# Halving the first input block by tokens over two DMA queues, and evacuating the first transposes in two pieces

## Chip, cores, metric

One core of a Trainium2 chip. The metric is device time in microseconds (us) of one execution, median of several. Times of the profiler's own span are about 1.8 us shorter than the device time and are used only to compare profiles.

## The reference, cut to what matters

Four layers on x of shape (1, 2048, 1024) in bf16: linear attention, gated MLP, and both again, each behind a layer norm.

```python
x = x + _A_ref(_layernorm(x), A_wqkv, A_wo)      # 32 heads, phi(q), phi(k), linear attention
x = x + _B_ref(_layernorm(x), B_W_gate, B_W_up, B_W_down)
...                                              # the same two once more
```

Only the very start matters here: the first tokens of x must be loaded, normalized, transposed, and multiplied with the first columns of `wqkv`.

## The kernel before

x is worked on in blocks of 128 tokens (one token per partition, 1024 columns). The head of the kernel loads block 0 in two column halves, one on SP's DMA queue and one on ScalarE's, and keeps TensorE (PE) busy with dummy matmuls meanwhile:

```python
def head(self):
    ...
    zero = self.ep.tile([P, NW], BF16, tag="e")
    nc.vector.memset(zero, 0.0)
    idle = self.ps3.tile([P, NW], F32, tag="b")
    for _ in range(12):
        nc.tensor.matmul(idle, lhsT=zero[:, 0:P], rhs=zero, start=True, stop=True)

    k0, k1, v0, q0, q1 = (ring.place() for _ in range(5))
    self.load_x(0, 0)                    # block 0, columns 0..511, SP's queue
    self.load_x(0, 1, nc.scalar)         # block 0, columns 512..1023, ScalarE's queue
    k0(0, H)                             # first half of the first weight block, SP
    self.load_x(1, None, nc.scalar)      # block 1, whole, ScalarE's queue
    k0(H, 2 * H)
    self.load_x(2)
    k1()
    ...
```

`k0(0, H)` is 512 rows of 1 KB, `load_x(1)` 128 rows of 2 KB. Four 128x128 transposes go into one PSUM tile, which is then copied to SBUF ("evacuated") by VectorE or ScalarE. The order of the first block on VectorE and ScalarE is written out by hand. `stat` takes the statistics of one half of a block, `rstd` makes the mean and the reciprocal standard deviation of them (VectorE's aggregate, then two steps on ScalarE), `scale` normalizes, `turn` transposes:

```python
def turn(j, h):
    tp = self.ps3.tile([P, H, P], BF16, tag="b")
    for i in range(H):
        kt = h * H + i
        nc.tensor.transpose(tp[:, i, :], xn[j][:, kt * P:(kt + 1) * P], self.ident)
    dst = self.xnT[0, 0][:, h * H:(h + 1) * H, j * P:(j + 1) * P]
    ...                                  # take(engine): copy tp to dst

def block0():
    stat(0, 0)                           # block 0: statistics of both column halves
    stat(0, 1)
    rstd(0)
    stat(1, 0)                           # block 1 stands ahead of block 0's scaling
    scale(0, 0)
    scale(0, 1)
    t0 = turn(0, 0)
    t1 = turn(0, 1)
    t0("s")
    stat(1, 1)
    rstd(1)
    t1("v")
    k(0, 0, between)                     # 8 matmuls; block 1's transposes after the sixth
```

## Time and profile before

| | before |
|---|---|
| device time, first three runs | 1629.09 us (1628.83 to 1629.37) |
| PE busy in the profiled span | 1621.9 of 1627.0 us |
| block 0's halves land | 3.43 and 3.61 us |
| block 1 lands | 5.26 us |
| block 0's scaling starts | 5.90 us |
| first projection matmul | 7.44 us |

Read it from the bottom up. PE is all but saturated after 7.44 us, so the time is what PE's work takes plus what passes before it gets going. What happens in the first 7.44 us is read in the chain of waits and the timeline; the lines are shown in the prediction. "Lands" is when all 16 DMA engines have reported: each of these loads has 16 reports in the trace, and its consumer waits for the last (VectorE starts 0.02 us after block 1's). In the profile's lines PE is TensorE, DVE VectorE, ACT ScalarE and SP SyncE; a q after the name marks the engine's sequencer, which issues loads. PEclk, the granted clock, is the share of its full clock that PE was given.

### The profile page before, as it was taken

The page shows a single profiled execution, that of the slowest core. Times are in us where ns is not written, and L with a number is a line of the kernel's source. Part 1 is how long each engine was busy: PE and PEld are TensorE (multiplying, and loading weights), DVE is VectorE, ACT ScalarE, POOL GpSimd, SP SyncE. Part 2 cuts the span into 40 slices and gives each one's busy share as a digit, 9 for nine tenths or more (in the row PEclk, how much of TensorE's full clock was granted, in tenths as well). Part 3 has the DMA queues.
Part 4 walks back from the last instruction along what each step waited for, and adds up shares of the span by engine and source line. Part 5 has one row for each costly group of instructions (what it writes and reads, how often), then busy time and mean ns, then how long its engine had stood idle before and what let it go on. Part 6 is the DMA issues. An engine that isn't in the chain of part 4 may idle for free.

```text
span 1627.0 us, 18776 instructions
## 1 busy us (share of the span) xinstructions
PE 1621.9 (100%) x7756; PEld 740.3 (46%) x7756; DVE 566.7 (35%) x940; ACT 331.8 (20%) x638; POOL 201.9 (12%) x134
## 2 busy tenths in 40 slices
PE   9999999999999999999999999999999999999999
PEld 4444444444444444444444444444444444444444
DVE  7845695213112212222264547932021112111211
ACT  6741212101110110111067312121011101101110
POOL 2349220000000000000023582100000000000000
PEclk9999999999999999999999999999999999999999
DMA  8313547447445445544560147464554454454452
GB/s 253 58 52 61 173 75 210 144 147 227 155 158 188 156 147 166 168 149 134 168 121 1 52 99 247 86 190 146 187 165 150 156 179 155 145 168 152 155 162 72
DMA packets 298246, 235.06 MB, mean 144 GB/s; under 512 B 101296, under 2 KB 294192, under 8 KB 298160
## 3 DMA queue, kind: packets, MB, share of 16 engines
q1 hardware_dynamic: 293120, 229.27, 48.0%
q10 hardware_dynamic: 5040, 4.59, 0.8%
q8 instruction: 60, 0.98, 0.2%
q14 instruction: 26, 0.21, 0.0%
HBM read 201.33 MB, written 8.39 MB: 129 GB/s over the span
## 4 chain that ended last, share of the span: by engine, by line
PE 98%; ACT 1%; DVE 1%; issue 0%; DMA 0%; DVEq 0%
PE pg L640 24%; PE pu L640 24%; PE acc L664 23%; PE ps L405 12%; PE ps L531 7%; PE ps L440 7%; PE kv L453 0%; PE acc_last L664 0%; ACT e L352 0%; DMA x<-in_A_x_dram 0%; ACT e L351 0%; PE fold L516 0%; DVE st L139 0%; ACT e L353 0%; DVE slab L359 0%
## 5 line engine op out<-in xcount | busy, mean ns | idle before, releaser
L640 PEld LDWEIGHTS <-t 128*128 128x128 bf16 x3584 | 350.7, 98 | 422.8
L640 PE MATMUL pg<-xnT,t 128*128 128x512 bf16 x1792 | 423.3, 379 | 0.0
L640 PE MATMUL pu<-xnT,t 128*128 128x512 bf16 x1792 | 423.3, 379 | 0.0
L664 PE MATMUL acc<-t,hT 128*128 128x512 bf16 x1764 | 382.5, 379 | 0.0
L646 DVE TENSOR_TENSOR hT<-pu,rg 128x512 bf16<-128x512 f32 x224 | 154.8, 691 | 572.1 <-PE pu L640 572.1
L645 ACT ACTIVATE rg<-pg 128x512 f32<-128x512 f32 x224 | 133.5, 596 | 737.3 <-PE pg L640 737.0
L664 PEld LDWEIGHTS <-hT 128*128 128x128 bf16 x1820 | 178.1, 98 | 209.0
L405 PE MATMUL ps<-t,xnT 128*128 128x512 bf16 x1024 | 224.1, 379 | 0.5 <-ACT xnT L268 0.4
L405 PEld LDWEIGHTS <-xnT 128*128 128x128 bf16 x1024 | 99.3, 98 | 120.2 <-issue 2.0
L531 PE MATMUL ps<-T,pqT 128*128 128x512 bf16 x512 | 111.2, 379 | 0.0
L146 ACT ACTIVATE rstd<-mv,eps 128x1 f32<-128x1 f32 x64 | 18.7, 294 | 333.8 <-DVE mv L144 333.6
L681 DVE TENSOR_TENSOR xo<-x,acc 128x512 bf16<-128x512 f32 x31 | 21.3, 688 | 170.3 <-PE acc L664 170.3
L484 POOL TENSOR_TENSOR prod<-pq,zrow 128x1024 f32<-128x1024 bf16 x32 | 68.0, 2124 | 85.9 <-DVE den L489 72.5
L139 DVE BATCH_NORM_STATS2 stats<-x 128x6 f32<-128x512 f32 (+1 forms) x120 | 78.0, 673 | 0.8
L531 PEld LDWEIGHTS <-pqT 128*128 128x128 bf16 x512 | 49.9, 98 | 60.4 <-issue 0.5
L420 POOL CAST ksum<-x 128x512 f32<-128x512 bf16 x2 | 1.7, 866 | 605.4 <-DVE x L359 605.4
L678 DVE TENSOR_TENSOR x<-x,acc 128x512 f32<-128x512 f32 x32 | 21.6, 674 | 138.5 <-PE acc L664 137.4
L422 POOL TENSOR_TENSOR ksum<-ksum,slab 128x512 f32<-128x512 f32 x46 | 54.0, 1182 | 84.6 <-DVE slab L359 75.1
L359 DVE SCALAR_TENSOR_TENSOR pq<-ps,e 128x512 bf16<-128x512 f32 x64 | 44.0, 688 | 53.9 <-ACT e L353 52.2
L496 POOL TENSOR_TENSOR pq<-pq,den 128x1024 bf16<-128x1024 bf16 x32 | 61.7, 1934 | 3.1 <-DVE den L491 3.1
L489 DVE TENSOR_REDUCE den<-prod 128x32 f32<-128x1024 f32 x32 | 38.9, 1217 | 53.9 <-POOL prod L484 53.9
L440 PE MATMUL ps<-slab,x 128*128 128x512 bf16 x256 | 56.6, 379 | 0.0
(57 smaller groups left out, 596.8 us busy)
## 6 DMA issues: line engine op xcount, KB each, us to landing
t<-in_B_W_gate_dram SPq DMA_DIRECT2D x56, 1024.0 KB, 7.0
t<-in_B_W_up_dram SPq DMA_DIRECT2D x56, 1024.0 KB, 5.4
t<-in_B_W_down_dram SPq DMA_DIRECT2D x64, 896.0 KB, 5.2
t<-in_A_wqkv_dram SPq DMA_DIRECT2D x11, 1024.0 KB, 5.1
t<-in_A_wo_dram SPq DMA_DIRECT2D x4, 1024.0 KB, 6.8
away<-x SPq DMA_DIRECT2D x8, 512.0 KB, 4.3
x<-away SPq DMA_DIRECT2D x8, 512.0 KB, 8.4
out_dram<-xo ACTq DMA_DIRECT2D x31, 128.0 KB, 2.3
```

The lines of the kernel that those rows point to most:

```text
L139: self.nc.vector.bn_stats(out=stats[:, c, :], in_=src[:, c * fmax:(c + 1) * fmax])
L359: nc.vector.scalar_tensor_tensor(out=out, in0=ps, scalar=0.0, in1=e, op0=ALU.max, op1=ALU.add)
L405: nc.tensor.matmul(by_row(ps), lhsT=self.xnT[l, l_q][:, kt, j * P:(j + 1) * P], rhs=w[:, kt, :].rearrange("p (b i d) -> p i b d", i=R, d=H ...
L422: nc.gpsimd.tensor_tensor(out=ksum[:, cols], in0=ksum[:, cols], in1=pk, op=ALU.add)
L440: nc.tensor.matmul(ps, lhsT=self.xn[l, t][:, d * P:(d + 1) * P], rhs=self.pk[l, t][:, h * NW:(h + 1) * NW], start=(t == 0), stop=(t == sel ...
L484: nc.gpsimd.tensor_tensor(out=prod, in0=pq_of[sc, j], in1=zrow, op=ALU.mult)
L496: nc.gpsimd.tensor_tensor(out=heads(pq), in0=heads(pq), in1=den[:, :].unsqueeze(2).to_broadcast([P, D // HD, HD]), op=ALU.mult)
L531: nc.tensor.matmul(ps, lhsT=pqT[sc][:, g, j * P:(j + 1) * P], rhs=T[g // 2][:, g % 2, n2 * NW:(n2 + 1) * NW], start=(g == 0), stop=(g == G ...
L640: nc.tensor.matmul(ps, lhsT=w[:, kt, fi * P:(fi + 1) * P], rhs=self.xnT[l, q][:, kt, :], start=(kt == 0), stop=(kt == KT - 1))
L645: nc.scalar.activation(out=rg, in_=pg, func=ACT.Relu)
L646: nc.vector.tensor_tensor(out=h[:, fi, :], in0=pu, in1=rg, op=ALU.mult)
L664: nc.tensor.matmul(ps[:, 0:n], lhsT=hT[ft // 4][:, ft % 4, j * P:(j + 1) * P], rhs=wd[:, k, i * n:(i + 1) * n], start=(ft == 0), stop=(ft ...
```

## The change

The intent: longer rows (2 KB and not 1 KB) for the first block, and a first matmul that waits for half an evacuation only.

```diff
-        self.load_x(0, 0)
-        self.load_x(0, 1, nc.scalar)
+        for i, queue in enumerate((nc.sync, nc.scalar)):
+            p = slice(i * P // 2, (i + 1) * P // 2)
+            queue.dma_start(out=self.xb[0][p, :], in_=self.x_v[p, 0, :])
 ...
                 if engine == "v":
                     nc.vector.tensor_copy(out=dst, in_=tp)
+                elif engine == "s":
+                    nc.scalar.activation(out=dst, in_=tp, func=ACT.Copy)
                 else:
-                    nc.scalar.activation(out=dst, in_=tp, func=ACT.Copy)
+                    for i in range(0, H, 2):
+                        nc.scalar.activation(out=dst[:, i:i + 2, :], in_=tp[:, i:i + 2, :],
+                                             func=ACT.Copy)
 ...
-            t0("s")
+            t0("ss")
```

## The prediction

> **What bounds the kernel now.** I read the page first, then the chain of waits in the first 60 us, then the timeline of the same stretch, then the DMA issues of the first microseconds.
>
> From the page of the kernel before:
>
> ```profile
> span 1627.0 us, 18776 instructions
> ...
> PE 1621.9 (100%) x7756; PEld 740.3 (46%) x7756; DVE 566.7 (35%) x940; ACT 331.8 (20%) x638; POOL 201.9 (12%) x134
> ...
> PE 98%; ACT 1%; DVE 1%; issue 0%; DMA 0%; DVEq 0%
> ```
>
> TensorE is busy for 1621.9 of 1627.0 us, and 98% of the chain that ended last is matmuls. 5.1 us of the span is not PE work. The view of PE's waits lists only three stalls with a releaser: 1.3 us before the first warm-up matmul, 0.2 us before the first transpose, 0.4 us before the first projection matmul. The rest is two gaps of about 0.1 us (at 17.3 and 42.2 us) and the tail after the last matmul, about 3 us. The change touches none of the layers, only the first 10 us, so whatever it gives comes out of the little before the first projection. Between 1.3 and 6.2 us PE runs twelve dummy matmuls: these count as busy, so the real wait of PE at the head is longer than its idle time says, and runs to 7.44 us.
>
> The chain of waits from 0 to 60 us (start us, us, what):
>
> ```profile
> 1.19 4.07 DMA x<-in_A_x_dram
> 5.26 0.02 issue
> 5.29 0.04 DVE st L139
> 5.32 0.57 issue
> 5.90 0.41 DVE x L155
> 6.30 0.05 issue
> 6.35 0.41 PE tp L261 x4
> 6.79 0.61 ACT xnT L268
> 7.39 0.05 issue
> 7.44 1.47 PE ps L405 x6
> 8.91 0.22 PE tp L261 x4
> ```
>
> The head's chain starts with a load issued at 1.19 us. That is not x block 0 (issued at 0.74 and 0.76 us) but x block 1. The reason is DVE's order: the statistics of block 1's first half stand ahead of the scaling of block 0. From there the chain is scale, four transposes, ScalarE's evacuation (0.61 us), first projection matmul at 7.44.
>
> Timeline from 0 to 40 us (start us, us, engine, line, operation, what ended the idle time):
>
> ```profile
> 3.46 1.29 DVE L139 BATCH_NORM_STATS2 st<-x 128x6 f32<-128x512 bf16 x2 [2.17 <-DMA x<-in_A_x_dram]
> ...
> 5.35 0.20 ACT L147 ACTIVATE rstd<-rstd 128x1 f32<-128x1 f32 x1
> ...
> 7.38 0.37 DVE L266 COPY xnT<-tp 128x512 bf16<-128x512 bf16 x1
> ...
> 7.50 0.29 ACT L146 ACTIVATE rstd<-mv,eps 128x1 f32<-128x1 f32 x1
> ...
> 8.06 0.74 DVE L155 TENSOR_SCALAR x<-x,mv,rstd 128x512 bf16<-128x512 bf16 x2 [0.31 <-ACT rstd L147]
> ```
>
> Block 0's statistics start at 3.46 us and its rstd is done at 5.55 us. Scaling could start at about 5.60; it starts at 5.90 because of block 1. So block 0 has **0.30 us of slack**.
>
> DMA issues between 1.15 and 1.25 us (KB each, us from issue to landing):
>
> ```profile
> x<-in_A_x_dram ACTq DMA_DIRECT2D x1, 256.0 KB, 4.1
> x<-in_A_x_dram ACTq DMA_DIRECT2D x1, 128.0 KB, 2.9
> ```
>
> ScalarE's half of block 0 lands at 0.76 + 2.9 = 3.7 us; the SP half, by the same view at its issue, at 0.74 + 2.7 = 3.4. Block 1 lands at 1.19 + 4.1 = 5.3.
>
> **What the Trainium skill says.** "ScalarE: Activation LUTs", section "What ACT_TABLE_LOAD costs": an ACTIVATE with immediate scale and bias takes 186 ns + 0.833 ns per column, and back-to-back ones overlap by about 93 ns. The trace agrees: the 128x512 evacuation takes 597 ns against 612, and the pair of them at 13.81 us takes 1.08 us, an overlap of 0.11. "SBUF — State Buffer", section "Door 1: The DMA port swizzle", says that partitions 0 to 63 reach 8 of 16 ports and 64 to 127 the other 8; its section on issuing two DMAs for both halves says that two such transfers together were only 6% faster than one. No transfer of the kernel before is of that shape, so its trace doesn't show it. "PSUM — Partial Sum Buffer", section "PSUM bank collisions raise a hardware error", says to guard PSUM by bank, not by address: so I take it that the first evacuation piece still waits for all four transposes. "DMA: Bandwidth & Descriptors", section "Queues, rings and completion order", says that each DMA engine alternates between the queues packet by packet. The trace fits: from 2.25 to 3.0 us queue 10 (ScalarE's) moved 132 packets and queue 1 (SP's) 119.
>
> **Part one, evacuation in two pieces.** It removes one ACTIVATE of 128x512 (0.60 us) and adds two of 128x256. By the formula each is an estimated 186 + 213 = 399 ns; scaled to the trace (597/612), 0.39. The first piece starts at 6.79 as before and ends at 7.18. PE needs 0.05 us from there (7.39 to 7.44 in the chain), so the first matmul moves from 7.44 to about 7.23: **0.21 us earlier**. The second piece overlaps the first by 0.1 and ends near 7.48. It feeds the third matmul, due at 7.23 + 2 x 0.216 = 7.66, so it is in time. The fifth matmul, at 8.09, needs VectorE's copy (done 7.75) and the second half of the first weight block (issued at 1.66, landed after 5.8, so 7.47): both in time.
>
> What else the second piece touches: ScalarE's rstd of block 1 starts at 7.50, when VectorE's aggregate is ready. The pieces end at about 7.48 instead of 7.39, so this is met by a hair; I allow 0 to 0.05 us.
>
> Does the gain last? After six matmuls PE transposes block 1, at 8.74. That input is ready when the first scaling at 8.06 is done: 8.06 + 0.41 + 0.05 = 8.52. PE would now be there at 8.53. So the gain is just kept; anything over 0.22 us would be lost here. From 9.56 the chain goes PE, VectorE's copy at 9.82, VectorE's norms, PE at 17.4, ScalarE's phi passes, PE at 42.3: each starts from what precedes it and moves along; none waits on a load with less room (block 2 landed at 2.2 + 6.0 = 8.2 and is read at 10.17; the second weight block landed at 2.75 + 8.4 = 11.2 and is due at about 11.3, close). After 42 us PE is never idle till the tail, so 0.2 us at the head is 0.2 us at the end. Part one: **-0.2 us**.
>
> **Part two, x block 0 by tokens.** Bytes and issues are the same, 128 KB on each queue; 256 packets of 1 KB become 128 of 2 KB. In the trace 1 KB packets take about 46 ns and block 1's 2 KB ones about 78 ns (138 packets, 46.5% of 16 engines over 1.5 us, is 81 ns), so per byte 2 KB rows are some 14% cheaper: 128 x 2 x 46 - 128 x 79 = 1.7 us of engine time, over 16 engines 0.1 us. Against this, now both statistics need both halves: before, the first started on the SP half at 3.46 and the other half came in behind it. At unchanged landings the statistics start at 3.7, 0.2 us later, and block 0 could be scaled at 5.60 + 0.2 = 5.80: still inside its 0.30 us slack. So by itself the change in block 0's landing costs and gives **nothing**, unless it lands after about 3.75. What could count is block 1, behind it on ScalarE's queue: each 0.1 us that it lands earlier is 0.1 us of the head, up to about 0.3, where block 0's rstd takes over. I credit the 0.1 us of cheaper packets with half, and hold the half-port risk against it: net **0, give or take 0.2**.
>
> Sum: 1629.09 - 0.2 - 0 = 1628.9 us.
>
> **Rivals.** First, the wait moves to the load. If two transfers that each write half of the ports run one after the other at an estimated 200 GB/s (the skill's 196 for that shape), 256 KB take 1.3 us from the first packet at 1.76 us, plus the 0.6 us from last packet to landing that I read for ScalarE's half (packets to about 3.0, landing 3.7): 3.7 us, on the edge of the slack. Somewhat worse, and both block 0 and block 1 slip by 0.2 to 0.4: the time would be 1629.0 to 1629.3. For it: the page's two sections. Against it: the old halves also took from 1.76 to about 3.0, so little is lost.
> Second, the load pays off: fewer, larger packets bring block 1 forward by 0.2 to 0.3 us, and everything on VectorE with it, including the scaling that caps part one. Then 1628.5 to 1628.6. For it: block 1 lands 1.6 us after block 0's half although it is only twice the size. Against it: 0.1 us is all the packet time that is saved.
> Third, the gain is swallowed: if rstd of block 1 is delayed by the second piece, or PE waits for block 1's scaling, part one gives 0 to 0.1 us and the time is 1629.0 to 1629.1.
>
> **Range and chances.** The three runs before spread over 0.54 us, as large as the whole effect. With -0.2 expected, about 0.3 of doubt in the mechanism and 0.2 in the measurement, I take 1628.9, with 1628.4 to 1629.4. 2% would be 32 us; the whole head is 7.4 us, so within 2% is all but sure: 0.996, and 0.002 for each side.
>
> **What would show each step.** Right: two ACT groups of 128x256 at about 0.39 us each; first projection matmul near 7.2 us; transposes of block 1 near 8.5; block 0's statistics at 3.4 to 3.75 and not on the chain; block 1's landing within 0.2 us of 5.3; PE busy time the same within 1 us; span 0.2 us shorter. Wrong: a chain that starts with block 0's load, statistics after 3.8 us, the first scaling moved from 5.90 by more than 0.2, an idle PE before block 1's transposes, or the first piece starting before 6.79 by more than the shift of the scaling, which would mean that it waits for two transposes and not four.

## The result

| | before | changed |
|---|---|---|
| median, 6 runs each | 1628.98 us (1628.76 to 1629.37) | **1631.91 us** (1631.49 to 1632.33) |
| ratio | | 1.0018, 95% interval 1.0005 to 1.0031 |

The ratio is the mean time of one kernel's runs over that of the other's of the same rounds, so not quite the ratio of the medians. Within 2% it is "the same"; but it is 2.9 us **slower**, over three times the spread of either kernel's runs, where 0.2 us faster was forecast. All 2.9 us can be found in the first 12 us.

From the page of the changed kernel:

```profile
span 1629.9 us, 18779 instructions
...
PE 1622.8 (100%) x7756; PEld 740.7 (45%) x7756; DVE 566.7 (35%) x940; ACT 331.7 (20%) x639; POOL 202.0 (12%) x134
```

PE has 0.9 us more busy time with the same 7756 instructions, and about 2 us more without work. Both need a cause. The chain of waits of the changed kernel, 0 to 60 us (start us, us, what):

```profile
1.39 5.68 DMA x<-in_A_x_dram
7.13 0.57 issue
7.70 0.41 DVE x L155
8.16 0.62 PE tp L262 x4
8.80 0.39 ACT xnT L272
9.24 2.53 PE ps L410 x6
11.77 0.22 PE tp L262 x4
```

Set it beside the chain of before. It is the same chain, starting with the same load (block 1), but that load lands at 7.07 and not at 5.26: **1.81 us later**. The scaling follows 1.80 us later (7.70 against 5.90). The four transposes take 0.62 and not 0.41. The evacuation takes 0.39 and not 0.61, as forecast; the first matmul comes at 9.24 against 7.44, so 1.80 later. Then six matmuls take 2.53 and not 1.47. The next transposes are 2.86 us late (11.77 against 8.91), and that stays: 1629.9 - 1627.0 = 2.9 us.

The timeline of the changed kernel, 4 to 12 us, VectorE and ScalarE (start us, us, engine, line, operation, count, what ended the idle time):

```profile
4.14 1.29 DVE L139 BATCH_NORM_STATS2 st<-x 128x6 f32<-128x512 bf16 x2 [2.86 <-DMA x<-in_A_x_dram]
...
7.09 0.69 DVE L139 BATCH_NORM_STATS2 st<-x 128x6 f32<-128x512 bf16 x1 [1.42 <-DMA x<-in_A_x_dram]
```

```profile
6.04 0.20 ACT L147 ACTIVATE rstd<-rstd 128x1 f32<-128x1 f32 x1
8.80 0.66 ACT L272 ACTIVATE xnT<-tp 128x256 bf16<-128x256 bf16 x2 [2.56 <-PE tp L262]
9.35 0.29 ACT L146 ACTIVATE rstd<-mv,eps 128x1 f32<-128x1 f32 x1
```

Block 0's statistics start at 4.14 and not 3.46, its rstd is done at 6.24, so its scaling would have been possible at 6.29. VectorE instead sits idle for 1.42 us before block 1's statistics at 7.09.

**Why is block 1 late?** DMA queues between 3.5 and 4.5 us (queue, packets, MB, share of 16 engines; q1 is SP's, q10 ScalarE's). Before:

```profile
q10 hardware_dynamic: 113, 0.23, 60.3%
q1 hardware_dynamic: 160, 0.16, 46.4%
```

Changed:

```profile
q1 hardware_dynamic: 326, 0.33, 107.5%
```

Before, block 1's rows (q10) and the weight rows (q1) go side by side. In the changed kernel not one row of ScalarE's queue moves in that microsecond; the engines are full of weight rows. Counted in the trace by start times, 239 of the 512 rows of the first weight half had started when the middle row of block 1 started before, and 514 weight rows (two of them of the next half) in the changed kernel: that whole half had started before it. Block 1's first packet starts at 4.68 us and not 3.13, 1.55 later, and its last packet starts 1.94 us after the first and not 1.60.

What differs where the two loads are issued? The timelines around 1.2 us before (start us, us of issue):

```profile
1.19 0.45 ACTq L370 DMA_DIRECT2D x<-in_A_x_dram  x1
```

```profile
1.19 0.42 SPq L35 DMA_DIRECT2D t<-in_A_wqkv_dram  x1
```

and around 1.4 us in the changed kernel:

```profile
1.38 0.57 SPq L35 DMA_DIRECT2D t<-in_A_wqkv_dram  x1
1.39 0.83 ACTq L375 DMA_DIRECT2D x<-in_A_x_dram  x1
```

Before, block 1 begins its issue 4 ns ahead of the weights and ends it 28 ns behind them. Changed, it begins 11 ns behind and ends 0.27 us behind. The issue of a half of block 0 itself takes 0.58 us as 64 rows and took 0.40 as 128 shorter ones. In e11 below, 128 rows of 2 KB took 0.40 as well, so the longer issue goes with the number of rows and not with their length. Block 0's first row moves at 2.11 us and not 1.76.

**Why is PE slow afterwards?** PE's waits in the changed kernel (us in total, times, longest) and its stretches of one us (length, PE busy, granted clock, DMA share, GB/s):

```profile
PE tp L262 <- DVE x L155: 2.5, 1, 2.5
```

```profile
core 0: us, PE busy (x), PEclk, DMA share, GB/s
...
6.00:7.00 1.00, 0.00 (x0) 1.00 1.07 350
7.00:8.00 1.00, 0.00 (x0) 1.00 1.03 371
8.00:9.00 1.00, 0.84 (x8) 0.50 1.08 382
9.00:10.00 1.00, 0.95 (x4) 0.50 1.08 358
```

The warm-up matmuls end at 5.70 us, the transposes start at 8.16. After the idle stretch the granted clock is 0.50 for 3.41 us, from about 8.0 to 11.4; matmuls start every 0.427 us and not every 0.216. Before, the clock is 1.00 in every such stretch from 6 to 11 us. Half clock for 3.41 us takes 0.001 off the mean clock of the whole span; all six runs of the changed kernel have a mean of 0.999, where the runs of the kernel before in the experiments have 1.000, so it most likely happened in all six. So the bill by the traces is 1.81 (late load) + 0.21 (transposes at half clock) - 0.22 (evacuation) + 1.06 (six matmuls at half clock) = 2.86 us. PE's busy time grew by less than these two slow parts, because the warm-up matmuls got shorter: the clock rose at 4.60 us and not at 5.50, so the twelve took 4.35 us and not 4.80. All eight transposes took 1.03 and not 0.72: 1.06 + 0.31 - 0.45 = 0.92 us.

### The profile page after: what moved, and what is told of

It is laid out like the page before. It is cut to its first block, busy times and chain, and to the rows that moved or that the text cites. A ratio compares the mean times of both kernels' runs of the same rounds, so it can differ in the third digit from the quotient of the medians.

```text
span 1629.9 us, 18779 instructions
## 1 busy us (share of the span) xinstructions
PE 1622.8 (100%) x7756; PEld 740.7 (45%) x7756; DVE 566.7 (35%) x940; ACT 331.7 (20%) x639; POOL 202.0 (12%) x134
## 3 DMA queue, kind: packets, MB, share of 16 engines
q10 hardware_dynamic: 4976, 4.59, 0.8%
## 4 chain that ended last, share of the span: by engine, by line
PE 98%; ACT 1%; DVE 1%; DMA 0%; issue 0%; DVEq 0%
PE pg L645 24%; PE pu L645 24%; PE acc L669 23%; PE ps L410 12%; PE ps L536 7%; PE ps L445 7%; PE kv L458 0%; PE acc_last L669 0%; DMA x<-in_A_x_dram 0%; ACT e L357 0%; ACT e L356 0%; PE fold L521 0%; DVE st L139 0%; ACT e L358 0%; DVE slab L364 0%
```

## Experiments

Theories at the outset. **Order:** block 1's load loses because the weights get ahead of it; token halves matter only through that. **Shape:** loads of 64 rows are slow or block the engines whatever the order. **Clock:** of the 2.9 us, some 1.2 are the half clock, a consequence of the idle stretch. Eleven kernels ran, all with correct results. "Landing" below is first to last of the 16 engines. The extra "small load" of two runs fills a tile that nothing reads:

| run | what | median us | before, same rounds |
|---|---|---|---|
| e1 | two pieces only | 1628.76 | 1629.19 |
| e2 | tokens only | 1632.49 | 1629.19 |
| e3 | changed, small load ahead of the weights | 1629.50 | 1629.19 |
| e4 | before, small load ahead of block 1 | 1633.97 | 1629.19 |
| e5 | changed, 22 warm-up matmuls | 1630.59 | 1629.09 |
| e6 | changed, weights' first quarter apart | 1629.67 | 1629.09 |
| e7 | changed, block 1 on SP first | 1630.40 | 1629.09 |
| e8 | e1, block 1 on SP first | 1629.16 | 1629.09 |
| e9 | e1, block 1 first on ScalarE's queue | 1629.43 | 1628.99 |
| e10 | changed, queues of block 1 and weights exchanged | 1630.88 | 1628.99 |
| e11 | block 0 whole on SP, block 1 on ScalarE's | 1629.39 | 1628.99 |

The interval of the ratio to the kernel before excludes 1 for e2 (1.0007 to 1.0034) and e4 (1.0014 to 1.0042) alone; smaller differences from it rest on the traces. The runs of e3, e5 and e6 all lie below those of the changed kernel.

### e1 and e2: each part alone

e1 is the changed kernel with the two `load_x(0, ...)` lines of before; e2 is the kernel before with the token halves.

```diff
 # e1                                             # e2 is the reverse, with t0("s") kept
-        for i, queue in enumerate((nc.sync, nc.scalar)):
-            p = slice(i * P // 2, (i + 1) * P // 2)
-            queue.dma_start(out=self.xb[0][p, :], in_=self.x_v[p, 0, :])
+        self.load_x(0, 0)
+        self.load_x(0, 1, nc.scalar)
```

> Part one alone: x block 0 by columns as before, evacuation in two pieces. My theory (the loss is all in the load part: block 1's load falls behind the first weight block): block 1 lands at 5.3 us as before, scaling at 5.90, first projection matmul at 7.2 instead of 7.44, time about 1628.8, 0.2 us under the kernel before. Rival that the two pieces themselves cost (a lost wait, a late rstd): 1629.1 or more.

Measured: 1628.76 us (1628.57 to 1628.96, 5 runs) against 1629.19 (1628.79 to 1629.57, 9 runs), ratio 0.9998, interval 0.9985 to 1.0010. From its chain of waits:

```profile
1.19 4.40 DMA x<-in_A_x_dram
...
7.11 0.39 ACT xnT L271
7.50 0.05 issue
7.55 1.47 PE ps L409 x6
```

In this profile block 1 landed at 5.59, 0.33 later than in that of before, yet the first matmul comes only 0.11 later: from the start of the evacuation to the first matmul it is 0.44 us, and 0.65 before. The part does what it should, 0.21 us. The medians differ by 0.43, with an interval of the ratio that includes 1; the trace is the better evidence for the size. It has the lowest median of all kernels run, but the runs do not show that it is faster than the kernel before.

> Part two alone: x block 0 by tokens, evacuation in one piece. My theory: block 1 lands near 7.1 us, PE idles about 2.5 us and runs at half clock for about 3.4 us after it, first projection matmul at about 9.4, time about 1632.1, that is 0.2 us over the changed kernel. Rival (loss from both parts together): clearly under 1631.9.

Measured: 1632.49 us (1632.07 to 1633.27), 3.3 over the kernel before. Block 1 lands from 5.81 to 7.43 us, 517 weight rows ahead of its middle row; six matmuls take 2.74 us at clock 0.50, which lasts 6.83 us here and not 3.41. The whole loss is in this part.

### e3 and e4: the order, mended and broken

The same small load, 16 rows of 1 KB, delays the weights in the changed kernel (e3) and block 1 in the kernel before (e4). Neither changes how block 0 is halved in its kernel.

```diff
         (the two loads of block 0, by tokens in e3, by columns in e4)
+        pad = self.const.tile([16, NW], BF16, name="pad")
+        nc.sync.dma_start(out=pad, in_=self.x_v[0:16, 0, 0:NW])      # e4: nc.scalar
```

> The changed kernel with one small load (16 rows of 1 KB) put on SP's queue ahead of the first weight block, so that this is issued some 0.4 us after block 1's load and not 11 ns before it. Theory 'order of issue': block 1 lands at 5.0 to 5.5 us, no half clock, time 1628.7 to 1629.1. Rival 'loads of 64 rows are slow or clog the engines, whatever the order': block 1 still lands near 7 us and the time stays near 1631.9.

Measured: 1629.50 us (1629.21 to 1629.90). The small load's 16 rows, and no weight row, went ahead of block 1's middle row; block 1 landed from 4.38 to 5.88 us, the clock was whole. Of the 2.9 us, 2.4 are gone with token halves still in place. The expected 1628.7 to 1629.1 was missed: five engines had reported by 4.50, the last eleven took from 5.11 to 5.88, and a later weight block, pushed back by the small load, cost PE another 0.3 us.

> The kernel before (by columns, one piece) with the same small load put on ScalarE's queue ahead of block 1's, so that block 1's load is issued about 0.4 us after the first weight block and not 4 ns before it. Theory 'order of issue': block 1 lands at 6.8 us or later, half clock at the first matmuls, time about 1632. Rival '64 rows': block 1 lands within 0.4 us of 5.3 and the time stays under 1629.6.

Measured: 1633.97 us (1632.45 to 1634.67). The kernel with column halves and one-piece evacuation becomes slower than the changed one:

```profile
1.66 6.08 DMA x<-in_A_x_dram
...
10.13 2.74 PE ps L407 x6
```

735 weight rows ahead, landing from 6.44 to 7.75 us, and the half clock. So 64-row loads are not needed for the loss, and undoing the order undoes most of it. It is more than the expected 1632: block 1 landed 0.3 us later than in e2, and the half clock lasted 6.83 us (7.97 to 14.80), so that the matmuls after the first six were slow too (the next two took 0.85 us and not 0.43). Three engines were late with block 0 as well (13 had reported by 3.54, the last at 4.59), but VectorE was done with its statistics at 5.95 and waited for block 1 until 7.77, so that is not on the chain.

### e5: the clock

```diff
-        for _ in range(12):
+        for _ in range(22):
```

> The changed kernel with 22 warm-up matmuls and not 12, so that PE stays busy until about 8 us and does not idle 2.5 us before the transposes. Theory (of the 2.9 us lost, 1.8 are the late load and about 1.2 the half clock after the idle stretch): block 1 still lands near 7.1 us, the first projection matmuls come every 0.216 us and not every 0.427, the clock is whole, time 1630.5 to 1630.9. Rival (the load alone costs all of it and PE's slowness is hidden behind it): time stays within 0.3 of 1631.9.

Measured: 1630.59 us (1630.20 to 1630.83), 1.3 under the changed kernel's 1631.91; the transposes and six matmuls at half clock had been 0.21 + 1.06 = 1.27. From its chain:

```profile
1.34 7.34 PE idle L221 x22
...
9.38 1.47 PE ps L410 x6
```

Block 1 landed no earlier (5.81 to 7.33 us) and the first matmul came 0.14 us later than in the changed kernel, but the matmuls run at full clock. The split of the loss is shown. Its timeline around 1.4 us brought something that I had not expected:

```profile
1.37 0.85 ACTq L375 DMA_DIRECT2D x<-in_A_x_dram  x1
1.38 0.57 SPq L35 DMA_DIRECT2D t<-in_A_wqkv_dram  x1
```

Here block 1 *began* its issue 8 ns ahead of the weights, and still 515 weight rows went first. So "who starts first" is not the rule in this trace. In all runs with token halves and a second load on ScalarE's queue, the issue of that load lasts 0.83 to 0.85 us; in the changed kernel, e2 and e5 it so ends 0.27 us after the weights', before and in e1 within 0.03, and in e3 and e6, where block 1 went ahead, before the issue of the bulk of the weights ends. That agrees with the end of the issue deciding, but no run takes the two apart further.

### e6: how much goes ahead

```diff
-        k0(0, H)
+        k0(0, 1)
+        k0(1, H)
         self.load_x(1, None, nc.scalar)
```

> The changed kernel with the first half of the first weight block cut into a quarter (128 rows of 1 KB) and three quarters (384 rows); block 1's load is then 11 ns behind 128 rows and no longer 11 ns behind 512. Theory 'block 1 waits until what was issued ahead of it has been drained': 384 rows fewer at about 80 per 0.25 us are 1.2 us, so block 1's first packets move from 4.5 us to about 3.4 and it lands at 5.7 to 6.1; the idle time of PE is then too short to lose the clock; time 1629.2 to 1630.0. Rival (it is the token halves themselves): near 7 us and 1631.9.

Measured: 1629.67 us (1629.47 to 1630.24).

```profile
1.39 4.84 DMA x<-in_A_x_dram
...
8.19 1.47 PE ps L411 x6
```

128 rows are issued ahead of block 1 and 138 went ahead of its middle row; first packet at 3.51 us and not 4.68. Fifteen engines reported by 5.57, the sixteenth at 6.23. PE idles 0.8 us before the transposes and keeps its clock. Taken together; with token halves the landing follows the rows ahead:

| run | halves | weight rows ahead of block 1's middle row | block 1's last landing, us | half clock |
|---|---|---|---|---|
| before | columns | 239, side by side | 5.26 | no |
| e1 | columns | 218, side by side | 5.59 | no |
| e3 | tokens | 0 (16 of the small load) | 5.88 | no |
| e6 | tokens | 138 | 6.23 | no |
| changed | tokens | 514 | 7.07 | yes |
| e5 | tokens | 515 | 7.33 | no (kept warm) |
| e2 | tokens | 517 | 7.43 | yes |
| e4 | columns | 735 | 7.75 | yes |

Both theories have a share: with few rows ahead block 1 lands early, but behind token halves it lands on ScalarE's queue at 5.88 or later even then (on SP's queue, in e7, at 4.64).

### e7 and e8: block 1 ahead by design

```diff
-        k0(0, H)
-        self.load_x(1, None, nc.scalar)
+        self.load_x(1)
+        k0(0, H)
```

> The changed kernel with block 1's load on SP's queue right behind block 0's half and ahead of the first weight block, so never behind it. Theory 'order of issue': first landings near 4.4 us, all by 5.0 to 5.9, no half clock, time 1628.5 to 1629.2. If token halves have a cost of their own (stragglers among the engines, as the run with the small load hints: landings from 4.4 to 5.9), it is over the same edit with columns by 0.2 us or more.

> Columns as before, evacuation in two pieces, block 1's load on SP's queue ahead of the first weight block. Order of block 1 and weights is then safe by design and not by 4 ns; block 1's landing at 5.0 to 5.6, time 1628.5 to 1629.0, within 0.3 us of the run with the two pieces alone, and under the kernel before. If ScalarE's queue is needed to bring block 1 early: 1629.2 or more.

Measured: e7 1630.40 us (1629.85 to 1631.72), e8 1629.16 (1628.94 to 1630.68). Block 1 does land early, by 4.64 and 4.47 us, but both expectations missed what comes next: the weights' first half lands by 8.65 in e7 and 8.48 in e8, where it was 5.73 before, and PE waits for it. In e8 fifteen of the 16 engines had reported by 6.57, so one late engine made 1.9 us of this; the profiled execution was the slowest of the five (1630.68, the others 1628.94 to 1629.59). Token halves are 1.2 us over columns here, by the medians.

The profiled execution of e7 was the slowest of its five too (1631.72, the others 1629.85 to 1630.64), and it lost the clock after two short waits and no long one. Its waits, its chain and one of its stretches:

```profile
PE ps L410 <- DMA t<-in_A_wqkv_dram: 1.2, 1, 1.2
PE tp L262 <- DVE x L155: 0.6, 1, 0.6
```

```profile
8.69 2.48 PE ps L410 x6
```

```profile
9.00:10.00 1.00, 1.00 (x4) 0.52 1.09 379
```

The other four runs of e7 have a mean clock of 1.000 and this one 0.999, so the same kernel can keep the clock or lose it.

### e9, e10, e11: looking for a better head

All keep the two-piece evacuation.

```diff
 # e9: columns                        # e10: tokens                       # e11
+  self.load_x(0, 0)                  +  (token halves)                   +  self.load_x(0)
+  self.load_x(1, None, nc.scalar)    +  self.load_x(1)                   +  self.load_x(1, None, nc.scalar)
+  self.load_x(0, 1)                  +  k0(0, H, nc.scalar)              +  k0(0, H)
+  k0(0, H)
```

> Looking for a version under both: two-piece evacuation, both column halves of block 0 on SP's queue, and block 1's load as the first on ScalarE's queue (issued near 0.76 us, ahead of every weight). Theory 'what counts is what is drained ahead of block 1': block 1 lands near 4.0 to 4.4, block 0's second half near 3.9; the statistics of block 1 no longer hold up block 0's scaling, which goes to 5.6 from 5.90 and is then set by block 0's own rstd; first projection matmul near 6.95; time 1628.3 to 1628.8. Rival (weights, now issued 0.5 us later, become the wait): first matmul waits on a weight load and the time is 1628.9 or more.

Measured: 1629.43 us (1629.11 to 1629.58). Block 1 landed at 3.93, as hoped, and the rival won:

```profile
PE ps L409 <- DMA t<-in_A_wqkv_dram: 0.6, 2, 0.5
```

The weights' second half, 7.47 us before, landed at 8.66.

> The changed kernel with block 1's load and the first weight half exchanged between the queues: block 1 on SP, the weights on ScalarE, both still issued about 10 ns apart. In the token runs the second issue on SP took 0.57 us and that on ScalarE 0.83, so block 1's now ends first. Theory 'what is handed over first is drained first, and the end of the issue tells it, not the start': block 1's landings from 4.2 to 4.9, weights from 5.2 to 6.2, time 1628.6 to 1629.3. Rival 'the start decides' gives the same here if block 1 starts first; rival 'ScalarE's queue yields to SP's whatever the order' too; rival 'token halves themselves delay what follows': block 1 after 6.5 and 1631 or more.

Measured: 1630.88 us (1629.47 to 1632.12). Block 1 landed from 4.20 to 5.50, ahead of the weights, as expected; the weights, now on ScalarE's queue with an issue of 0.83 us, landed from 5.64 to 8.75:

```profile
1.39 7.36 DMA t<-in_A_wqkv_dram
```

Thirteen engines had reported by 6.79. PE waited 1.5 us and kept its clock in the profiled execution (1630.14 us). The two slowest of the four runs (1631.62 and 1632.12) have a mean clock of 0.999, as the changed kernel's have, so there it was most likely lost. The time was missed by over 1.5 us.

> 2 KB rows without halves: block 0 in one load of 128 rows on SP's queue, block 1 at the same time on ScalarE's, two-piece evacuation. Theory: both land at 3.7 to 4.3 (512 KB at about 360 GB/s from 1.9 us, plus half a microsecond), statistics start about 4.0, scaling at about 6.1, first matmul at about 7.4, time 1628.9 to 1629.3. Rival (the two big loads share the engines unevenly, as token halves did): landings spread over more than 1 us, time over 1629.5.

Measured: 1629.39 us (1629.14 to 1629.72). Both blocks landed, at 4.46 and 4.69, within 0.46 us from first engine to last, where block 1 behind token halves took 1.2 to 1.6 us on ScalarE's queue (the halves themselves took 0.40 and 0.42 in the changed kernel); but block 0's own statistics are now the chain, the scaling comes at 6.61, and the kernel is 0.4 us over the one before.

## Why the prediction was wrong, point by point

- **What bounds the kernel** was right: the chain started with block 1's load, and what the head lost (2.86 us) is what the span lost (2.9). "0.2 us at the head is 0.2 us at the end" held in the other direction.
- **Part one** was right in mechanism and size: pieces of 0.38 us against 0.39, first matmul 0.21 us closer to the evacuation's start. The first piece waited for all four transposes: the fourth ended at 8.77, it started at 8.81. Block 1's rstd started 0.08 us after its aggregate and not 0.04: the 0.04 us more lie inside the 0 to 0.05 that were allowed.
- **Part two failed**, at "Bytes and issues are the same", and at "net 0, give or take 0.2" for block 1. Bytes were the same, issues were not: 0.58 us each and not 0.40, and the next one on ScalarE's queue 0.83 and not 0.45. I took it from the page ("DMA: Bandwidth & Descriptors", section "Queues, rings and completion order") that the engines alternate between queues packet by packet, read the trace's packets, which are single rows, as the page's, and so treated block 1's place as given. The page's packet is typically 9 to 17 descriptors and at most 64; the 512 weight rows over 16 engines are an estimated 32 each, if each row is one descriptor, so the page left room for what happened. Before, with the two issues ending within 0.03 us of each other, block 1 moved side by side with the weight rows; changed, with its issue ending 0.27 us later, it moved after them. That term measured +1.81 us in place of 0.
- **Block 0's own landing** was judged on the edge of its slack, 3.75 us. It came at 4.05 (3.53 for the other half), so even with block 1 on time the scaling would not have been possible before 6.29, 0.4 us after 5.90. The halves' packets were credited with saving time; the later of them landed 0.43 us later than before. The credit itself was too high: the 138 packets that it divides by include 11 of 4 bytes, and the 127 rows took 87 ns in the mean, so its sum is 128 x 2 x 46 - 128 x 87 = 0.6 us of engine time, 0.04 us over 16 engines and not 0.1.
- **The first rival** came nearest (a load takes the place of the evacuation, and block 1 slips), with the wrong size: 0.2 to 0.4 us of slip for block 1 where it was 1.8. It looked at how two halves share ports, not at what is drained between block 0 and block 1.
- **Missing altogether** was the step from "PE waits longer" to "PE runs at half clock". I had noted that the dummy matmuls end just before the transposes, and not asked what happens if the transposes slip by two microseconds. It cost 1.27 us by the trace and 1.3 in e5. The Trainium skill, "TensorE: Matmul & The Clock Gate", section "Part 1: The HAM clock gate", has PE fall to half clock after an idle window of about 3.4 us; here 2.46 us of idle were followed by 3.41 us at 0.50 (more on this in the last section).
- **The range** was too narrow by these two terms. Its width allowed about 0.3 us for the mechanism and 0.2 for the noise, and not that a head in which two issues end within 0.03 us of each other can tip.

What stays open: why an issue of 64 rows, and the issue after it, takes longer; whether its end is what decides; and why single engines report 0.5 to 2 us after the rest in several runs (in e8, one of 16).

## What to carry to other kernels

Before moving a load at the head of a kernel, list every load that is issued within half a microsecond of it, on every queue, and ask what happens if their order tips: here the bytes ahead of the critical load counted, not its own. Check also how long the dummy matmuls cover: here the first real work slipped 2.46 us past them, PE started at half clock, and a load that came 1.81 us late cost 2.9 us in all. A shorter slip can do the same (1.76 us of idle time in two waits in e7), and it can differ from run to run. When two parts are packed into one change, run each alone: the two-piece evacuation, alone, does in its trace what was forecast, and was hidden by the loss of the other part.

## What the Trainium skill lacked or had wrong

- "DMA: Bandwidth & Descriptors" (section "Queues, rings and completion order"): it has engines alternate between queues by whole packets, but does not say which of two loads issued at nearly the same time goes first. In the changed kernel no packet of ScalarE's queue moved from 3.5 to 4.5 us while 326 of SP's did, although the two issues began within 11 ns (514 weight rows ahead against 239 before).
- The same page gives no issue time by shape: 0.58 us for 64 rows of 2 KB against 0.40 for 128 rows of 1 KB or of 2 KB, and 0.83 against 0.45 for the same next load on ScalarE's queue.
- The same page (section "Latency and other measured facts") speaks of slow engines only for engines 7 and 15, and guesses at a cause in loads issued from GpSimd. Here loads issued from SP had a single late engine: in e8, fifteen of 16 engines reported by 6.57 us and the last at 8.48. The trace that was kept does not say which engine it was.
- "TensorE: Matmul & The Clock Gate" (Part 1): its idle window of about 3.4 us before the half clock is too long as a rule of safety. In these traces the clock changes lie 3.413 us or a multiple of it apart (4.60, 8.01 and 11.42 us in the changed kernel). Cut the traces into stretches of 3.413 us on that grid and take those that PE began at full clock: the half clock followed those in which PE idled 2.3 us (changed, e2 and e4) and 1.76 us (e7: waits of 0.60 and 1.16), and did not follow those with 1.55 us (e8), 1.49 us (e10's profiled run) or less. Where between 1.55 and 1.76 us the border lies, and whether it holds elsewhere, is not shown.
- "SBUF — State Buffer" (section on issuing two DMAs for both halves): nothing to correct. It says that two loads of 64 partitions gain only 6% over one; no run here has a single such load, so the 6% is not tested. The two together landed by 4.05 us, against 3.61 for the same bytes in 128-partition loads, but block 0's first row also moved 0.35 us later.
